# Attention with beacons, then a three-way maxout FFN: pair loads over 128 partitions, and three loads moved between queues and steps

## The chip, the cores and the metric

One Trainium2 chip; the kernel runs on one of its cores. The metric is device time in microseconds (us), read as the median of several runs of the whole kernel; lower is better. Within the core, TensorE (PE) multiplies, VectorE (DVE), ScalarE (ACT) and GpSimd (POOL) work on what it needs and leaves, and SyncE (SP) mostly issues transfers. Each engine takes its own instructions strictly in program order, so an instruction that waits holds back everything behind it on that engine. Transfers (DMAs) are issued from the queues of SP, ACT and POOL and are carried by 16 DMA engines that all queues share.

## The reference

Eight batches, eight heads, 576 tokens of width 64, and 16 beacon tokens per head that every query may see. The output of the attention, 4608 tokens by 512, goes through a maxout FFN.

```python
k_all = np.concatenate([beacon_k, k], axis=2)
v_all = np.concatenate([beacon_v, v], axis=2)
scores = scale * np.matmul(q, k_all.transpose(0, 1, 3, 2))
...
scores = np.where(causal, -1000000000.0, scores)
scores = scores - scores.max(-1, keepdims=True)
a = np.exp(scores)
a /= a.sum(-1, keepdims=True) + 1e-09
return np.matmul(a, v_all).astype(np.float32)
...
h = np.maximum(np.maximum(x @ w1, x @ w2), x @ w3)
return (h @ w_out).astype(np.float32)
```

All inputs and the output are float32 in memory. Here S is 576, Nb (beacons) 16, D 64, and the FFN goes 512 to 768 to 512.

## The kernel before

**The order is written out by hand.** The kernel turns off the scheduler's own choice of order (`manual_schedule`); what stands first in the code is issued first on its engine. The unit of attention work is a *pair* of heads: 32 pairs, four per batch. A pair's scores come in four groups (0 to 3). Two pairs make a *quad*, which is multiplied with the values in two halves (`emit_pv(quad, half)`). FFN work comes in 22 units per block of 512 tokens (`mm1_halves`, `mm1_unit`, `mm2_unit`), and `emit_ffn` slips them between the attention steps up to a running limit.

**How q and k come in.** In batch 0, halves and quads of heads are loaded (`load_half`, `load_quad`) and turned on TensorE (`turn_half`). In batches 1 to 3 (pairs 4 to 15, `B_PE = 4`) a pair is loaded in float32 by `load_pair` on SP's queue: token `6p + r` goes to partition `p` of 96, so one descriptor carries 6 tokens, 1536 bytes. POOL turns it into bf16 with two casts (`cast_pair`, `cast_piece`, line 218), TensorE turns it with 6 transposes for q and 6 for k (`turn`, line 347, each 96 columns), and the result is copied out of PSUM, k by DVE (`evac_k`, line 394) and q by ACT (`evac_q`, line 383; for pair 4 by DVE). From batch 4 on, pairs are stored in bf16 and come back through transposing DMAs; the change does not alter that route.

**How the values come in.** `load_v(b, piece)` loads a batch's values as tiles of 128 keys, descriptors of 256 bytes: piece 0 has tiles 0 to 2 and the 16 beacon rows, piece 1 has tiles 3 and 4. POOL casts them (line 275 for batch 0, line 263 later).

**Weights.** `load_w(i, ...)` (line 285) and `load_w_out` (line 290) are issued on POOL's own queue and cast from float32 to bf16 on the way. Each `load_w` is two DMAs.

**The first stage.** `start()` and the list `first_steps` set batch 0's order: `T` turns a half, `M` masks, `V` casts a value tile, `P` multiplies with the values, `F` emits FFN units, `G(p)` loads a pair behind a one-column memset on DVE that acts as a gate. `load_v(0, 1)` has such a gate too. `idle` is a number of filler transposes that `turn_half` puts before the second of its two parts, and `keep_busy` issues filler matmuls; neither result is used.

**Around the change**, POOL's order from 29 us on is: casts of pair 4, third weight (two DMAs), casts of pair 5, masks of pair 4, casts of pair 6, masks of pairs 4 and 5, cast of batch 1's first values (step (5, 0)), `load_w_out`, two masks of pair 5, cast of the other values, casts of pair 7, masks of pair 6. TensorE's order at step (6, 0) is: scores of pair 6, the product of quad 2 with the values (needs pair 5's masks), one FFN unit, the transposes of pair 7, and then the first FFN unit that reads the third weight. The output weight is first read by the first `mm2_unit`, at step (8, 0), line 620.

**SP's order** there is: pair 4, pair 5 (both gated), pair 6, batch 1's values in six DMAs, pair 7, then batch 2. A DMA of SP or ACT takes one of eight semaphores in turn, and waits for the DMA eight places before it.

```python
groups_any = [
    [(0, 0, HALF), (3, q_min[3], S)],
    [(0, HALF, S), (4, q_min[4], S)],
    [(1, q_min[1], S)],
    [(2, q_min[2], S)],
]
...
for p in range(8, B_PE * PPB):
    at_step(p - 2, 1, C(cast_pair, p, by_pool, by_pool))
```

Of the kernel before, what the change touches and what calls it, by code (L numbers as in the profile page):

```python
# [16 lines left out]
def kernel(  # L17
# [28 lines left out]

    QR = 6
    QP = S // QR
    HR = QR // 2
    HALF = S // 2  # L50

# [53 lines left out]
    def place(p):  # L105
        b, pi = divmod(p, PPB)
        return b, pi // PPQ, 2 * (pi % PPQ)
# [36 lines left out]
    qTs = [const.tile([128, S], BF16, name=f"qT{i}") for i in range(NT)]  # L144
    kTs = []
    for i in range(NT):
        z = const.tile([128, NKP], BF16, name=f"kT{i}")
        nc.vector.memset(z[:, NK:NKP], 0.0)
        nc.vector.memset(z[:, Nb + HALF : 384], 0.0)
        kTs.append(z)  # L150
# [20 lines left out]

    def load_pair(p, gate=None):
        b, g, j0 = place(p)
        hs = slice(head(g, j0), head(g, j0) + 2)
        st = new_stage(("pair", p))

        if gate:
            gate.memset(st[0:QP, 0:1], 0.0)
        for i, src in enumerate((q, k)):
            nc.sync.dma_start(  # L180
                out=st[0:QP, i * NQ2 : (i + 1) * NQ2].rearrange("p (h x) -> p h x", h=2),
                in_=src[b, hs].rearrange("h (p r) d -> p h (r d)", r=QR),
            )
# [31 lines left out]
    def cast_piece(p, i, cast):  # L215
        st = stage["pair", p]
        t16 = pair_pool.tile([QP, QR, 2, D], BF16, name=f"p16{i}")
        cast(  # L218
            t16.rearrange("p r h d -> p h r d"),
            st[0:QP, i * NQ2 : (i + 1) * NQ2].rearrange("p (h r d) -> p h r d", h=2, r=QR),  # L220
        )
        stage["pair16", p, i] = t16

    def cast_pair(p, q_cast, k_cast):
        cast_piece(p, 0, q_cast)
        cast_piece(p, 1, k_cast)
        stage.pop(("pair", p))
# [3 lines left out]
    def load_v(b, piece, gate=None):  # L231
        st = new_stage(("v", b, piece))
        if gate:
            gate.memset(st[0:QP, 0:1], 0.0)
        t_lo, t_hi = V_PIECES[piece]
        for t in range(t_lo, t_hi):
            i = t - t_lo
            dst = st[:, i * H * D : (i + 1) * H * D].rearrange("p (h d) -> p h d", h=H)
            lo = 0
            if t == 0:  # L240
                lo = Nb
                nc.sync.dma_start(
                    out=dst[0:Nb], in_=beacon_v[b].rearrange("h n d -> n h d")
                )
            t0 = k_tok[t] + lo
            n = k_rows[t] - lo
            nc.sync.dma_start(
                out=dst[lo : lo + n], in_=v[b, :, t0 : t0 + n, :].rearrange("h p d -> p h d")
            )
# [94 lines left out]
    def turn(p, i, ps):  # L344
        src = stage.pop(("pair16", p, i))
        for r in range(QR):
            nc.tensor.transpose(  # L347
                ps[:, r * QP : (r + 1) * QP],
                src[:, r].rearrange("p h d -> p (h d)"),
                ident[0:QP, 0:QP],  # L350
            )

# [29 lines left out]
    def evac_q(p, ps, copy):  # L382
        copy(
            qTs[p % NT].rearrange("d (p r) -> d p r", r=QR),
            ps.rearrange("d (r p) -> d p r", r=QR),
        )
# [5 lines left out]
    def evac_k(p, ps, copy):  # L392
        kT = kTs[p % NT]
        copy(
            kT[:, Nb:NK].rearrange("d (p r) -> d p r", r=QR),
            ps.rearrange("d (r p) -> d p r", r=QR),
        )

    def turn_apart(p, i):
        ps = ffn_psum.tile([128, S], BF16, name="fps")  # L400
        turn(p, i, ps)
        (evac_q, evac_k)[i](p, ps, by_dve)
        if i == 1:
            place_beacons(p, by_act)

    def turn_pair(p, q_copy, shared=True):
        if shared:
            ps = sc_psum.tile([128, 2, 1024], BF16, name="sc")
            banks = [ps[:, i, 0:S] for i in range(2)]
        else:  # L410
            banks = [pv_bank(i, [128, 1024], BF16)[:, 0:S] for i in range(2)]
        for i in range(2):
            turn(p, i, banks[i])
        evac_k(p, banks[1], by_dve)
        evac_q(p, banks[0], q_copy)
# [286 lines left out]
    loads = [L(load_v, 0, 0), L(load_v, 0, 1, nc.vector), L(load_beacons, 1, B_PE, bk32_1)]  # L702
# [18 lines left out]
    def start():  # L721
# [25 lines left out]
        keep_busy(3)  # L747
# [41 lines left out]
    def F(n):  # L789
# [7 lines left out]
        ((2, 0), [T(0, 1, False, None, 6), next_2, V(2), L(load_w, 0, 0, d_ff)]),  # L797
        ((3, 0), [T(1, 1, True, None, 8), M(1, 0, True), M(2, 0, True)]),
        ((0, 1), [M(0, 1)]),
        ((0, 2), [T(2, 1, False), M(3, 0, True), M(0, 2), V(3), V(4)]),  # L800
        ((0, 3), [M(0, 3, True), L(load_w, 1, 0, d_ff)]),
        ((1, 1), [P(0, 0), M(1, 1)]),
        ((1, 2), [T(3, 1, False), finish_pv, M(1, 2)]),
        ((1, 3), [P(1, 0, True), M(1, 3, True)]),
        ((2, 1), [finish_pv, G(4), cast_p]),
# [4 lines left out]
        ((3, 3), [F(2), M(3, 3), L(cast_pair, 4, by_pool, by_pool), L(load_w, 2, 0, d_ff), P(1, 1),  # L810
# [4 lines left out]
    at_step(5, 0, L(load_w_out))  # L815
    at_step(5, 1, C(cast_v, 1, 1, by_pool))
    at_step(5, 1, C(cast_pair, 7, by_pool, by_pool))
    for p in range(8, B_PE * PPB):
        at_step(p - 2, 1, C(cast_pair, p, by_pool, by_pool))
# [127 lines left out]
```

## Time and profile before

| | |
|---|---|
| median of 6 runs | 301.66 us |
| lowest and highest run | 300.61 and 307.27 us |
| the profiled execution's own time | 300.54 us |
| span of that execution in the trace | 298.8 us |
| PE busy | 282.8 us (95%) |
| PE weight loads, beside the matmuls | 153.1 us (51%) |
| DVE, ACT, POOL busy | 173.1, 146.3, 128.2 us |
| DMA moved | 50.68 MB in 85320 packets, mean 170 GB/s |
| share of packets under 512 bytes | 64416 of 85320 |

A line of the trace's timeline reads: start, length (both in us from the span's start), engine, line of the kernel, operation, output tile <- input tile, shape, count, and in brackets the idle time of the engine just before it and what ended it. A line of the list of waits reads: who waited, for whom, total us, how many times, the longest. The chain of waits is followed back from the end of the span; each piece is the work that released the next. The granted TensorE clock is full in all parts of the span.

### The profile page before, as it was taken

What the parts mean: (1) busy time and instruction counts of PE and PEld (TensorE: products, weight loads), DVE (VectorE), ACT (ScalarE), POOL (GpSimd) and SP (SyncE); (2) the same over time, 40 slices, a digit from 0 to 9 for tenths busy, and PEclk for the clock granted to TensorE, in tenths of its full rate; (3) what the DMA queues carried; (4) which work ended last, traced back from release to release, by engine and by line L of the source; (5) the groups of instructions that cost most, each with busy time, mean ns of one, the idle gap of its engine ahead of it and who ended that gap; (6) DMA issues with size and microseconds to landing.
All of it is one profiled execution on the core that took longest, in us unless ns stands there. A gap on an engine that the chain in (4) does not pass through costs nothing.

```text
span 298.8 us, 8667 instructions
## 1 busy us (share of the span) xinstructions
PE 282.8 (95%) x3571; PEld 153.1 (51%) x3601; DVE 173.1 (58%) x343; ACT 146.3 (49%) x237; POOL 128.2 (43%) x253
## 2 busy tenths in 40 slices
PE   8879977999999999999999999999999999999995
PEld 4546644554545454444545777545454554444442
DVE  3756644455767576646563757375746575284373
ACT  3685574875665465546453646364635431401300
POOL 7181856666475684456455645552233210000000
PEclk9999999999999999999999999999999999999999
DMA  8999989999999999999999999983111001103003
GB/s 146 186 184 232 216 187 265 250 224 296 231 234 240 189 312 206 194 195 318 223 186 220 316 226 186 162 263 82 42 67 76 2 3 73 69 1 128 14 0 141
DMA packets 85320, 50.68 MB, mean 170 GB/s; under 512 B 64416, under 2 KB 80032, under 8 KB 85280
## 3 DMA queue, kind: packets, MB, share of 16 engines
q1 hardware_dynamic: 80672, 45.76, 69.1%
q0 software_dynamic: 4048, 4.03, 8.2%
q8 instruction: 28, 0.46, 0.7%
q10 hardware_dynamic: 560, 0.33, 0.5%
q14 instruction: 12, 0.10, 0.1%
HBM read 35.13 MB, written 14.22 MB: 165 GB/s over the span
## 4 chain that ended last, share of the span: by engine, by line
PE 81%; DMA 9%; POOL 3%; DVE 2%; ACT 2%; issue 1%; SPq 0%; POOLq 0%; DVEq 0%
PE fps L584 31%; PE sc L584 12%; PE pv L524 11%; PE fps L620 11%; PE sc L452 8%; PE sc L620 4%; DMA st<-in_v_dram 4%; DMA quad<-in_k_dram 3%; DMA st<-in_k_dram 2%; PE sc L347 2%; ACT at_sb L461 1%; DVE xT L556 1%; POOL v_sb L263 1%; POOL quad L209 1%; DVE y L628 1%
## 5 line engine op out<-in xcount | busy, mean ns | idle before, releaser
L461 ACT ACTIVATE at_sb<-sc 128x928 bf16<-128x928 f32 (+5 forms) x128 | 103.8, 861 | 83.9 <-PE sc L452 83.2
L584 PE MATMUL fps<-xT,w_sb 128*128 128x512 bf16 (+1 forms) x464 | 106.4, 356 | 2.1 <-issue 0.8
L480 POOL TENSOR_SCALAR_AFFINE_SELECT at_sb<-at_sb 128x256 bf16<-128x256 bf16 (+2 forms) x148 | 53.9, 383 | 97.2 <-ACT at_sb L461 97.2
L584 PEld LDWEIGHTS <-w_sb 128*128 128x128 bf16 x672 | 61.7, 98 | 65.3 <-issue 12.2
L594 DVE TENSOR_TENSOR hT<-hT,fps 128x512 bf16<-128x512 bf16 x70 | 48.0, 687 | 29.4 <-PE fps L584 29.0
L218 POOL CAST p<-st 96x768 bf16<-96x768 f32 x56 | 44.7, 822 | 1.1 <-DVE hT L613 0.6
L584 PE MATMUL sc<-xT,w_sb 128*128 128x512 bf16 (+1 forms) x187 | 42.9, 356 | 0.1
L452 PE MATMUL sc<-qT,kT 64*128 64x288 bf16 (+5 forms) x400 | 35.9, 277 | 2.4 <-ACT at_sb L461 2.0
L620 PE MATMUL fps<-w_out_sb,hT 128*128 128x512 bf16 x143 | 34.6, 379 | 0.9 <-issue 0.6
L620 PEld LDWEIGHTS <-hT 128*128 128x128 bf16 x210 | 19.8, 98 | 24.1 <-DVE hT L594 2.1
L594 DVE TENSOR_TENSOR hT<-hT,sc 128x512 bf16<-128x512 bf16 x32 | 22.0, 688 | 16.9 <-PE sc L584 11.3
L628 DVE COPY y<-fps 128x512 f32<-128x512 f32 x25 | 17.3, 692 | 23.5 <-PE fps L620 23.5
L592 DVE CAST hT<-fps 128x512 bf16<-128x512 f32 x32 | 22.1, 692 | 12.3 <-PE fps L584 12.2
L556 DVE TENSOR_TENSOR xT<-pv,recip 128x288 bf16<-128x288 f32 (+2 forms) x93 | 27.3, 349 | 2.7 <-ACT recip L546 2.7
L524 PE MATMUL pv<-at_sb,v_sb 128*32 128x288 bf16 (+5 forms) x1376 | 28.7, 229 | 0.0
L452 PEld LDWEIGHTS <-kT 64*128 64x128 bf16 x400 | 14.4, 94 | 26.7 <-issue 22.1
L524 PEld LDWEIGHTS <-v_sb 128*32 128x32 bf16 (+1 forms) x1408 | 24.4, 96 | 2.0 <-issue 0.6
L524 PE MATMUL pv<-at_sb,ones 128*32 128x288 bf16 (+4 forms) x500 | 17.5, 256 | 2.5 <-POOL at_sb L480 2.4
L263 POOL CAST v_sb<-st 128x1536 bf16<-128x1536 f32 (+2 forms) x21 | 18.4, 893 | 3.0 <-DMA st<-in_v_dram 3.0
L544 ACT ACTIVATE lnd<-pv 128x288 f32<-128x288 f32 x31 | 12.9, 416 | 10.0 <-PE pv L524 10.0
L524 PEld LDWEIGHTS <-ones 128*32 128x32 bf16 (+2 forms) x512 | 10.9, 95 | 9.8 <-issue 8.2
L592 ACT CAST hT<-sc 128x512 bf16<-128x512 f32 x6 | 3.5, 586 | 23.7 <-PE sc L584 23.7
(74 smaller groups left out, 163.0 us busy)
## 6 DMA issues: line engine op xcount, KB each, us to landing
out_dram<-y SPq DMA_DIRECT2D x35, 256.0 KB, 3.2
st<-in_q_dram SPq DMA_DIRECT2D x28, 288.0 KB, 5.8
st<-in_k_dram SPq DMA_DIRECT2D x28, 288.0 KB, 6.4
st<-in_v_dram SPq DMA_DIRECT2D x24, 256.0 KB, 5.6
w_sb<-in_moe_w_dram POOLq DMA_DIRECT2D x6, 384.0 KB, 7.3
q_dram<-p SPq DMA_DIRECT2D x16, 144.0 KB, 2.9
k_dram<-p SPq DMA_DIRECT2D x16, 144.0 KB, 2.9
st<-in_v_dram SPq DMA_DIRECT2D x8, 224.0 KB, 6.2
```

What stands on the lines that cost most here:

```text
L218: cast(t16.rearrange("p r h d -> p h r d"), st[0:QP, i * NQ2 : (i + 1) * NQ2].rearrange("p (h r d) -> p h r d", h=2, r=QR),)
L263: cast(v_sb[0:n, t:t1].rearrange("p t h d -> p (t h d)"), st[0:n, (t - t_lo) * H * D : (t1 - t_lo) * H * D],)
L452: nc.tensor.matmul(ps[:, e, off : off + q1 - q0], kT[hs, 128 * t : 128 * t + 128], qT[hs, q0:q1], start=True, stop=True, tile_position=(64 ...
L461: nc.scalar.activation(out=both_heads(p, gi), in_=ps[:, :, 0 : g_width(p, gi)], func=AF.Exp, scale=scale)
L480: nc.gpsimd.affine_select(out=view, in_=view, compare_op=ALU.is_ge, fill=0.0, base=x0, pattern=[[0, 2], [1, hi - lo]], channel_multiplier=-1,)
L524: nc.tensor.matmul(ps[bank][32 * j : 32 * j + 32, lo + q0 - qa : lo + qb - qa], lhsT, at_view(PPQ * quad + j // 2, t, j % 2, q0, qb), star ...
L556: nc.vector.tensor_mul(xT[:, 2 * g + part - 1, c0 + ca : c0 + cb], ps[bank][:, lo : lo + cb - ca], recip[:, ca:cb],)
L584: nc.tensor.matmul(ps[:, o0 : o0 + n], w_in[i][:, ct, 128 * ft : 128 * (ft + 1)], xT[:, ct, x0 : x0 + n], start=(ct == 0), stop=(ct == n_c ...
L592: (by_act if alone[0] else by_dve)(h, ps)
L594: nc.vector.tensor_max(h, h, ps)
L620: nc.tensor.matmul(ps, hT[:, ft, 128 * tt : 128 * (tt + 1)], w_out_sb[:, ft, :], start=(ft == 0), stop=(ft == n_ft - 1),)
L628: nc.vector.tensor_copy(y, ps)
```

## The change

Pairs of batches 1 to 3 are loaded over 128 partitions: tokens 0 to 511 as `4p + r` (1024 bytes a descriptor), and the remaining 64 tokens of q and of k in one square, q on partitions 0 to 63, k on 64 to 127 (256 bytes a descriptor). That is 4 DMAs for a pair in place of 2, 3 casts in place of 2, 9 transposes of 128 columns in place of 12 of 96, and one copy more out of PSUM: the square's two halves go to the ends of q and k in one strided copy, for which qT and kT become parts of one tile. q's copy has 512 columns in place of 576.

The third weight is issued at step (4, 1), behind the masks of pair 4, in place of step (3, 3); the output weight at step (6, 0) in place of (5, 0). In batch 0 the second value tile is issued on ScalarE's queue, and in every batch the beacon rows come behind the first value tile. P(1, 0) moves behind the scores (2, 1). The fillers grow: one matmul, and 2 + 8 + 8 transposes.

```diff
+    WR = 4
+    WIDE = 128 * WR
+    REST = S - WIDE
...
-    qTs = [const.tile([128, S], BF16, name=f"qT{i}") for i in range(NT)]
-    kTs = []
...
+    qkTs = [const.tile([128, S + NKP], BF16, name=f"qkT{i}") for i in range(NT)]
+    qTs = [z[:, 0:S] for z in qkTs]
+    kTs = [z[:, S : S + NKP] for z in qkTs]
...
+    def load_wide(p, gate=None):
+        b, g, j0 = place(p)
+        hs = slice(head(g, j0), head(g, j0) + 2)
+        st = new_stage(("pair", p))
+
+        if gate:
+            gate.memset(st[:, 0:1], 0.0)
+        W = 2 * WR * D
+        for i, src in enumerate((q, k)):
+            nc.sync.dma_start(
+                out=st[:, i * W : (i + 1) * W].rearrange("p (h x) -> p h x", h=2),
+                in_=src[b, hs, 0:WIDE].rearrange("h (p r) d -> p h (r d)", r=WR),
+            )
+        for i, src in enumerate((q, k)):
+            nc.sync.dma_start(
+                out=st[REST * i : REST * (i + 1), 2 * W : 2 * W + 2 * D].rearrange("p (h d) -> p h d", h=2),
+                in_=src[b, hs, WIDE:S].rearrange("h p d -> p h d"),
+            )
...
+    def cast_wide(p, cast):
+        st = stage.pop(("pair", p))
+        t16 = pair_pool.tile([128, 2 * QR, 2, D], BF16, name="p16")
+        W = 2 * WR * D
+        for i in range(2):
+            cast(
+                t16[:, WR * i : WR * (i + 1)].rearrange("p r h d -> p h r d"),
+                st[:, i * W : (i + 1) * W].rearrange("p (h r d) -> p h r d", h=2, r=WR),
+            )
+        cast(t16[:, 2 * WR].rearrange("p h d -> p (h d)"), st[:, 2 * W : 2 * W + 2 * D])
+        stage["wide16", p] = t16
...
-    def load_v(b, piece, gate=None):
+    def load_v(b, piece, gate=None, queues=None):
...
+            (queues[i] if queues else nc.sync).dma_start(
+                out=dst[lo : lo + n], in_=v[b, :, t0 : t0 + n, :].rearrange("h p d -> p h d")
+            )
...
     def turn(p, i, ps):
-        src = stage.pop(("pair16", p, i))
-        for r in range(QR):
+
+        src = stage["wide16", p]
+        slots = [(r, WR * i + r) for r in range(WR)] + ([(WR, 2 * WR)] if i == 1 else [])
+        for r, slot in slots:
             nc.tensor.transpose(
...
     def evac_k(p, ps, copy):
...
         copy(
-            kT[:, Nb:NK].rearrange("d (p r) -> d p r", r=QR),
-            ps.rearrange("d (r p) -> d p r", r=QR),
+            kTs[p % NT][:, Nb : Nb + WIDE].rearrange("d (p r) -> d p r", r=WR),
+            ps[:, 0:WIDE].rearrange("d (r p) -> d p r", r=WR),
         )
+        step = S + Nb
+        x0 = S + NKP - 2 * step
+        copy(
+            qkTs[p % NT][:, x0:].rearrange("d (i x) -> d i x", i=2)[:, :, WIDE - x0 : S - x0],
+            ps[:, WIDE : WIDE + 2 * REST].rearrange("d (i x) -> d i x", i=2),
+        )
...
-    loads = [L(load_v, 0, 0), L(load_v, 0, 1, nc.vector), L(load_beacons, 1, B_PE, bk32_1)]
+    loads = [L(load_v, 0, 0, None, (nc.sync, nc.scalar, nc.sync)), L(load_v, 0, 1, nc.vector), L(load_beacons, 1, B_PE, bk32_1)]
...
-        keep_busy(3)
+        keep_busy(4)
...
-        ((2, 0), [T(0, 1, False, None, 6), next_2, V(2), L(load_w, 0, 0, d_ff)]),
+        ((2, 0), [T(0, 1, False, None, 8), next_2, V(2), L(load_w, 0, 0, d_ff)]),
...
-        ((0, 2), [T(2, 1, False), M(3, 0, True), M(0, 2), V(3), V(4)]),
+        ((0, 2), [T(2, 1, False, None, 8), M(3, 0, True), M(0, 2), V(3), V(4)]),
...
-        ((1, 2), [T(3, 1, False), finish_pv, M(1, 2)]),
-        ((1, 3), [P(1, 0, True), M(1, 3, True)]),
-        ((2, 1), [finish_pv, G(4), cast_p]),
+        ((1, 2), [T(3, 1, False, None, 8), finish_pv, M(1, 2)]),
+        ((1, 3), [M(1, 3, True)]),
+        ((2, 1), [P(1, 0, True), finish_pv, G(4), cast_p]),
...
-        ((3, 3), [F(2), M(3, 3), L(cast_pair, 4, by_pool, by_pool), L(load_w, 2, 0, d_ff), P(1, 1),
+        ((3, 3), [F(2), M(3, 3), L(cast_pair, 4, by_pool, by_pool), P(1, 1),
...
-    at_step(5, 0, L(load_w_out))
+    at_step(4, 1, L(load_w, 2, 0, d_ff))
...
+    at_step(6, 0, L(load_w_out))
```

## The prediction, on record before the changed kernel was run

> **What bounds the kernel now.** I read the page's table of busy time first, then the chain of waits, then the timelines of TensorE, GpSimd and SyncE where the chain leaves TensorE.
>
> ```profile
> PE 282.8 (95%) x3571; PEld 153.1 (51%) x3601; DVE 173.1 (58%) x343; ACT 146.3 (49%) x237; POOL 128.2 (43%) x253
> ...
> PE 81%; DMA 9%; POOL 3%; DVE 2%; ACT 2%; issue 1%; SPq 0%; POOLq 0%; DVEq 0%
> ```
>
> TensorE does the work that ends last: in the timeline four 512-column matmuls of the FFN take 0.86 us, one behind the other. So a change helps only where TensorE stands still, or where it gets less to do. From 60 us to the end its gaps over 0.15 us are some 0.16 each. The chain leaves it for long in one place, before 51 us:
>
> ```profile
> 23.49 7.44 DMA st<-in_k_dram
> 30.94 11.59 DMA st<-in_v_dram
> 42.68 1.46 POOL v_sb L263
> 44.14 0.79 POOL w_out_sb L290
> 44.94 0.77 POOL at_sb L480 x2
> ```
>
> Batch 1's values land at 42.6 us, POOL casts them, issues the output weight, and only then masks pair 5, for which TensorE waits. The same in the timelines (POOL, then PE, then SP):
>
> ```profile
> 31.75 1.08 POOL L285 DMA_DIRECT2D w_sb<-in_moe_w_dram  x2
> ...
> 38.69 1.01 POOL L480 TENSOR_SCALAR_AFFINE_SELECT at_sb<-at_sb 128x224 bf16<-128x224 bf16 x3 [0.41 <-ACT at_sb L461]
> 42.68 1.46 POOL L263 CAST v_sb<-st 128x1536 bf16<-128x1536 f32 x1 [2.98 <-DMA st<-in_v_dram]
> ```
> ```profile
> 45.41 0.55 PE L524 MATMUL pv<-at_sb,ones 128*32 128x176 bf16 x6 [2.35 <-POOL at_sb L480]
> ...
> 47.64 0.43 PE L347 MATMUL sc<-ident,p 96*128 96x96 bf16 x6 [0.24 <-POOL p L218]
> 48.50 0.43 PE L347 MATMUL sc<-ident,p 96*128 96x96 bf16 x6 [0.44 <-POOL p L218]
> ```
> ```profile
> 29.33 11.59 SPq L247 DMA_DIRECT2D st<-in_v_dram  x5
> 40.97 1.01 SPq L180 DMA_DIRECT2D st<-in_q_dram  x1
> ```
>
> Five value DMAs need 11.59 us to be issued, while the third weight, issued at 31.75, is moving. In the trace's packets its 256 are carried from 34.6 to 41.0 us and take 64.2 us of engine time, over 16 engines 4.0 us. From 37 to 38 us the engines began 66 of them and no packet of the values. That is what the change attacks.
>
> **The third weight moves (step (4, 1)).** Without its 4.0 us the first values land at 42.55 - 4.0 = 38.6. POOL reaches the weight's issue at 38.3 (end of pair 4's masks, 37.52 + 0.76), spends 1.08 on it, masks pair 5 until 40.4 and casts the values until 41.9 (1.46): it no longer waits for them. Pair 5's last two groups leave ACT at about 41.7 and 42.4, POOL masks them by 42.8, and the wait of 2.35 at 45.41 is gone. Next in line is pair 7. POOL casts the other values (1.16) by 44.0 and pair 7 by 45.5; TensorE, which ended pair 7's transposes at 48.93, could end them at 46.0. That is the upper end, a gain of 2.9. It needs pair 7 in SBUF by 45.2, and now the third weight runs against pair 7. Its first packets came 1.3 us (first weight) to 2.9 us (third) behind the issue, so from 39.6 to 41.2. If pair 7 is shut out as the values were, it lands when values, pair 7 and weight are all through. Pair 6 lands at 35.6 in the trace; a 256 KB value tile lands 1.1 to 1.2 us behind the one before (at 61 to 63 us), 4.6 tiles make 5.3; pair 7 takes 2.3 (two landings, 1.15 apart, in pairs 4 to 6); with the weight's 4.0 that is 47.2, and POOL's last cast (0.29, below) lets TensorE end at 48.0: a gain of 0.9, the lower end. It can be better, since SP now gets to pair 7 some 2 us earlier (its issue at 40.97 stood behind the values' issue, and from 41 to 42 us the engines were busy 0.48). I take 2.1 between the two: the three weights' issues are followed by gaps nearer 2.9 than 1.3 when the queue is full, which favours pair 7.
>
> **The output weight (step (6, 0)).** It is issued behind pair 6's masks (1.01), so at about 46.7 instead of 44.08, and took 13.7 us to land. TensorE reads it at 60.72, and 2.1 earlier if the gain holds: 58.6. With 13.7 it would land at 60.4, a wait of 1.8; that is one end. Of the 13.7, 4.3 passed before its first packet and 8.5 with packets alternating with pair loads of 1536 bytes (78 ns in the median, its own 97). Two thirds of a pair's packets now have 1024 bytes and one third 256 (18 ns); scaled by bytes from 78, 52 and 18 average 41, and 48 rounds of 97 + 41 give 6.6: landing at 57.9, no wait, the other end. I take 0.2, near the second end, since that one has the packets that the new kernel moves.
>
> **Loads over 128 partitions.** Per pair and engine: before 24 packets of 78 ns, 1.87 us; after 32 of 52 and 16 of 18, 1.95. Nothing gained by that; I take 0 (-0.3 to +0.3 for each of pairs 4 to 7), hidden behind the prefetch of 8 stage tiles later on (pair 8 landed at 49.7, cast at 52.4). SP issues two DMAs more per pair, 0.45 us each: 0.9 us for 12 pairs, covered as long as four issues (1.8) stay under a pair's 2.3. The casts: 610 ns for 128x512 (row of the values' cast) twice and, from 610 and 1459 for 1536 columns, about 290 for 128 columns: 1.51 against 2 x 822 = 1.64.
>
> Two sentences of the Trainium skill speak against this part. "DMA: Bandwidth & Descriptors", section "Rules for kernel authors", advises to merge small transfers, since under 64 KB overhead is most of the cost; the two new DMAs have 32 KB each. The trace agrees half: a 32 KB beacon DMA takes 4.9 us to land and a 256 KB tile 5.6, but several are in flight at once. By the rule, with its fixed cost as an estimate of 2 us for each, pair 7 would come 4 us later and the sum would be a loss of about 2.
>
> **Transposes and copies.** Filler transposes have 128 columns too: 6 take 0.51 and 8 take 0.62, so 55 ns each; 96 columns: 6 take 0.43 and 12 take 0.68, so 42. Nine of 55 are 495 ns, twelve of 42 are 504: nothing. DVE's copy: 754 ns for 576 columns and 454 for 288, so 687 for 512 and 287 for 128: 0.22 more per pair, and ACT (640 for 576, 400 for 288, so 587 for 512) starts behind it. Both lie under FFN units that follow the transposes (98.39, 3.83 us), except for pair 7, where scores waited 0.35 for ACT's copy. I take +0.1 (0 to 0.2 for one pair; 9 x 0.17 = 1.5 if the cover were gone).
>
> **The first 23 us.** A value tile of 256 KB goes to ACT's queue, its issue (0.45) under ACT's wait of 2.35 before 4.44. Then two queues of values alternate with the quads of q and k on POOL's queue, where before it was one; TensorE waits for a quad three times (0.49 at 9.05, 0.39 at 12.04, 0.27 at 14.72). Lower end 0, upper end the tile's own 1.2. Against it, scores (2, 1) ahead of P(1, 0) give ACT back its 0.43 of idle before 20.38. The fillers, 18 x 55 ns and one matmul of 0.3, lie in those waits and in 0.38 and 0.93 for ACT; the cost is their 1.3 if the waits were gone. Sum 0.1 (-0.4 to +0.9). If the delay is large, values and first weight overlap more, POOL's last cast of values and behind it the second weight come later.
>
> The same page, same section, has it that spreading DMAs over several queues gains no bandwidth, only issue time. By that rule the move is worth SP's 0.44 us of issue, which nothing waits for, and the sum would be unchanged.
>
> **The sum.** -2.1 + 0.2 + 0 + 0.1 + 0.1 = -1.7 on the profiled execution: 300.54 - 1.7 = 298.8 (span 297.1). That execution lies 1.1 under the median of the runs shown, 301.66; I keep the distance and forecast a median of 301.66 - 1.7, rounded to 299.9.
>
> **Rivals.**
> 1. *The stall only changes its place.* Pair 7 lands at 47.2 (gain 0.9), the output weight is issued 1.5 later and lands late by 1, the first 23 us lose 0.5: 301.66 - 0.9 + 1.0 + 0.5, about 302.2, taken as 301.0 to 302.9. For it: DMA share is about 1.0 or over from 20 to 200 us save 41 to 46. Against it: just that stretch is free to be used.
> 2. *Slower: the output weight.* If pair 7 lands at 47.2, POOL casts until 47.5, masks until 48.5 and only then issues it; with 13.7 it lands at 62.2, 1.5 behind the 60.72 of before, with all earlier gains swallowed, and with the start's 0.9 not recovered separately. It decides from an issue after 47.0 (60.72 - 13.7). Time 301.66 + 1.5 to 3, about 303.5. For it: a slack of only 3.0 before (landed 57.7). Against it: the shorter packets beside it.
> 3. *The move doesn't do what it says:* the values don't land earlier because SP's eight semaphores hold pair 6 until pair 4 has landed (29.7; before, it was issued at 26.95). Then pair 6 is 1 us late, the gain 1 smaller: 300.9. It counts with rival 1.
>
> **How the numbers follow.** Forecast (a gain of 1.5 to 3.2, 298.5 to 300.2) 0.50; rivals 1 and 3 0.25; rival 2 0.25. A measurement of this kernel tells about 0.5% (1.5 us) from no change: faster 0.52, with a little of rival 3; same 0.22; slower 0.26. The forecast's own range is 298.5 to 300.3; reaching to the other cases, 298.2 to 303.2.
>
> **What would show it.** Right: POOL's cast at L263 begins near 40.4 with no wait for a DMA, PE's wait of 2.35 is gone, and pair 7's transposes end before 47. Wrong: a wait of PE over 1 us on a weight (the first `mm1_unit` with the third, or the first `mm2_unit`), on pair 7's casts, or quads that land over 1 us later; and any new gaps behind 60 us, where I cost the whole change at nothing.

## The result and the profile after

| | before | after |
|---|---|---|
| median of all runs | 301.37 us (69 runs) | 307.1 us (34 runs) |
| lowest run | 299.75 us | 301.26 us |
| ratio after / before | | 1.0068 (95% interval 1.0045 to 1.0092) |
| the profiled execution's own time, its span | 300.54, 298.8 us | 305.86, 304.1 us |

The forecast was 299.9 (298.2 to 303.2); the change makes the kernel slower, by 0.7% in the comparison. Executions of both kernels scatter upward by several us, of the new one more often, and the ratio leaves disturbed ones out, so it is smaller than the distance of the medians.

The page of the kernel after: busy time, granted clock in 40 slices, and the chain of waits by engine.

```profile
PE 286.2 (94%) x3554; PEld 155.5 (51%) x3584; DVE 173.9 (57%) x355; ACT 145.6 (48%) x237; POOL 125.8 (41%) x265
...
PEclk9997999999997999999999999999999999999999
...
PE 78%; DMA 9%; POOL 4%; DVE 3%; ACT 2%; SPq 2%; issue 2%; POOLq 0%; DVEq 0%; ACTq 0%
```

TensorE's share of the chain fell from 81 to 78%, POOL's rose from 3 to 4, and SP's queue, which had none, has 2. The clock was lowered in two slices. First the place that the change aimed at, in the timelines of POOL and of TensorE after:

```profile
41.41 1.08 POOL L322 DMA_DIRECT2D w_sb<-in_moe_w_dram  x2
42.49 1.02 POOL L526 TENSOR_SCALAR_AFFINE_SELECT at_sb<-at_sb 128x224 bf16<-128x224 bf16 x3
43.45 1.46 POOL L300 CAST v_sb<-st 128x1536 bf16<-128x1536 f32 x1
```
```profile
45.96 0.41 PE L570 MATMUL pv<-at_sb,ones 128*32 128x288 bf16 x12
...
49.84 0.61 PE L630 MATMUL fps<-xT,w_sb 128*128 128x512 bf16 x2 [0.76 <-DMA w_sb<-in_moe_w_dram]
```

The cast of batch 1's first values waits for nothing, and the 2.35 us at this product (45.41 before) are gone. But TensorE comes to this place 3.3 us later than before (26th exponent in the table below), and the weight itself is now waited for. The 3.3 us come from the start (POOL, then TensorE):

```profile
17.48 0.60 POOL L312 CAST v_sb<-st 128x512 bf16<-128x512 f32 x1
22.27 0.61 POOL L312 CAST v_sb<-st 80x512 bf16<-80x512 f32 x1 [4.19 <-DMA st<-in_v_dram]
22.83 1.08 POOL L322 DMA_DIRECT2D w_sb<-in_moe_w_dram  x2
```
```profile
24.39 0.52 PE L570 MATMUL pv<-at_sb,ones 128*32 128x208 bf16 x6 [1.92 <-POOL at_sb L526]
```

POOL stands 4.19 us at the cast of the last value tile (it landed at 22.2, before at 18.1); behind it are the second weight (18.87 before) and the masks for which TensorE waits. The clock is at half in the 3.4 us that follow. The second loss lies where the prediction saw nothing (POOL, then TensorE):

```profile
80.61 0.29 POOL L250 CAST p<-st 128x128 bf16<-128x128 f32 x1
88.10 0.61 POOL L740 CAST bk<-bk 64x512 bf16<-64x512 f32 x1 [7.19 <-DMA bk<-in_beacon_k_dram]
88.66 1.01 POOL L526 TENSOR_SCALAR_AFFINE_SELECT at_sb<-at_sb 128x224 bf16<-128x224 bf16 x3
89.62 1.75 POOL L261 CAST p<-st 96x768 bf16<-96x768 f32 x2
91.33 0.76 POOL L526 TENSOR_SCALAR_AFFINE_SELECT at_sb<-at_sb 128x256 bf16<-128x256 bf16 x2
```
```profile
91.78 0.56 PE L570 MATMUL pv<-at_sb,ones 128*32 128x176 bf16 x6 [2.40 <-POOL at_sb L526]
...
95.36 1.88 PE L630 MATMUL fps<-xT,w_sb 128*128 128x512 bf16 x6
```

POOL waits 7.19 us for the beacons of batches 4 to 7 (before 3.00, at 83.55), the masks behind it are late, TensorE waits, and then runs at half clock (six of these matmuls take 1.46 us at full clock). Why the beacons are late is seen in SP's timeline, first before, then after:

```profile
61.86 1.01 SPq L180 DMA_DIRECT2D st<-in_q_dram  x1
62.91 0.45 SPq L180 DMA_DIRECT2D st<-in_k_dram  x1
...
66.95 0.31 SPq L180 DMA_DIRECT2D st<-in_k_dram  x1
...
78.81 2.26 SPq L296 DMA_DIRECT2D bk<-in_beacon_k_dram  x4
```
```profile
64.63 0.47 SPq L185 DMA_DIRECT2D st<-in_q_dram  x1
65.15 0.47 SPq L185 DMA_DIRECT2D st<-in_k_dram  x1
65.66 0.60 SPq L190 DMA_DIRECT2D st<-in_q_dram  x1
66.31 0.60 SPq L190 DMA_DIRECT2D st<-in_k_dram  x1
...
75.73 0.61 SPq L190 DMA_DIRECT2D st<-in_k_dram  x1
...
82.75 3.29 SPq L333 DMA_DIRECT2D bk<-in_beacon_k_dram  x4
```

Pairs 12 to 15 took SP 5.4 us (61.86 to 67.26: eight loads and one store) and take 11.7 (64.63 to 76.34: sixteen loads and one store, each issue 0.47 to 0.61 us long but for one of 1.44). The turn of the eight semaphores is not what holds SP here: at each of these seventeen issues the DMA eight places before had landed at least 0.5 us earlier. The transfers have room meanwhile, as the table by stage says for 70 to 80 us (the last two numbers: share of the 16 DMA engines, GB/s), before and after:

```profile
70.00:80.00 10.00, 9.78 (x103) 4.57 (x104) 7.36 (x16) 6.14 (x10) 6.24 (x13) 1.00 1.13 284
```
```profile
70.00:80.00 10.00, 9.79 (x100) 4.67 (x101) 7.51 (x16) 6.24 (x10) 5.50 (x13) 1.00 0.72 216
```

To see where time is lost, take one thing that every kernel does equally often: ScalarE's 128 exponents. The table has, for each profiled execution, how much later (or earlier, -) than in the kernel before the 16th, 26th, 28th, 50th and 52nd of them ended; the times before were 28.86, 43.97, 51.97, 89.59 and 93.88 us. From the 52nd to the 128th the difference moves by 0.05 us at most in every kernel: all that is lost or gained is so before the 52nd.

| kernel | 16th | 26th | 28th | 50th | 52nd | median, its before | ratio (95%) |
|---|---|---|---|---|---|---|---|
| after, first profile | 3.43 | 3.27 | 0.38 | 0.54 | 5.69 | 307.1, 301.37 | 1.0068 (1.0045-1.0092) |
| r0_after | 0.67 | 0.90 | -1.52 | -1.36 | 1.75 | 305.47, 300.95 | 1.0114 (1.0064-1.0164) |
| e1_v_on_act | 5.14 | 5.15 | 3.70 | 3.70 | 4.29 | 305.72, 300.95 | 1.0160 (1.0116-1.0204) |
| e2_weights | 3.08 | 3.09 | 4.85 | 6.20 | 6.20 | 302.66, 300.95 | 1.0033 (1.0003-1.0063) |
| e3_wide | -0.34 | 2.33 | 0.98 | 1.13 | 4.38 | 305.56, 300.95 | 1.0140 (1.0108-1.0172) |
| e4_bk_early | 0.99 | 0.83 | -0.95 | 0.59 | 3.89 | 307.13, 301.4 | 1.0154 (1.0094-1.0214) |
| e5_v_on_sp | 0.21 | 0.05 | 0.78 | 0.95 | 5.00 | 302.73, 301.4 | 1.0054 (1.0024-1.0083) |
| e6_split | 1.71 | 1.71 | 3.85 | 4.68 | 4.67 | 303.23, 301.4 | 1.0058 (1.0017-1.0100) |
| e7_wide_weights_bk | 3.72 | 3.56 | 3.01 | 3.58 | 8.91 | 308.28, 301.4 | 1.0187 (1.0144-1.0230) |
| e8_rest_by_batch | -0.30 | -0.46 | -0.55 | 1.24 | 1.23 | 301.76, 302.91 | 0.9972 (0.9937-1.0007) |
| e9_casts_later | -0.36 | -0.52 | -0.30 | 2.40 | 2.39 | 301.8, 302.91 | 0.9982 (0.9939-1.0026) |
| e10_both | -0.05 | -0.21 | -0.95 | -0.78 | -0.80 | 301.28, 302.91 | 0.9915 (0.9863-0.9966) |
| e11_third_earlier | 6.75 | 6.69 | 4.46 | 4.62 | 4.61 | 301.23, 301.91 | 0.9965 (0.9937-0.9992) |
| e12_pair8_held | 3.69 | 3.54 | 3.15 | 5.07 | 5.06 | 299.46, 301.31 | 0.9935 (0.9902-0.9969) |
| e13_both_again | 0.10 | -0.06 | -2.28 | -2.12 | -2.13 | 301.13, 301.31 | 0.9956 (0.9918-0.9993) |

### The profile page after: what moved, and what is told of

It is laid out like the page before. It is cut to its first block, busy times and chain, and to the rows that moved or that the text cites. A ratio compares the mean times of both kernels' runs of the same rounds, so it can differ in the third digit from the quotient of the medians.

```text
span 304.1 us, 8661 instructions
## 1 busy us (share of the span) xinstructions
PE 286.2 (94%) x3554; PEld 155.5 (51%) x3584; DVE 173.9 (57%) x355; ACT 145.6 (48%) x237; POOL 125.8 (41%) x265
## 4 chain that ended last, share of the span: by engine, by line
PE 78%; DMA 9%; POOL 4%; DVE 3%; ACT 2%; SPq 2%; issue 2%; POOLq 0%; DVEq 0%; ACTq 0%
PE fps L630 29%; PE sc L630 12%; PE pv L570 11%; PE fps L666 10%; PE sc L498 7%; PE sc L666 4%; DMA quad<-in_k_dram 3%; DMA st<-in_v_dram 3%; DMA w_sb<-in_moe_w_dram 3%; PE fps L649 2%; ACT at_sb L507 1%; POOL at_sb L526 1%; PE sc L386 1%; SPq L333 1%; DMA bk<-in_beacon_k_dram 1%
## 5 line engine op out<-in xcount | busy, mean ns | idle before, releaser
L630 PE MATMUL fps<-xT,w_sb 128*128 128x512 bf16 (+1 forms) x464 | 107.5, 358 | 2.9 <-issue 1.0
L498 PE MATMUL sc<-qkT 64*128 64x288 bf16 (+5 forms) x400 | 35.9, 278 | 1.4 <-ACT at_sb L507 1.2
L638 DVE CAST hT<-fps 128x512 bf16<-128x512 f32 x32 | 22.1, 691 | 12.1 <-PE fps L630 11.9
L498 PEld LDWEIGHTS <-qkT 64*128 64x128 bf16 x400 | 14.6, 94 | 25.8 <-issue 21.6
L261 POOL CAST p<-st 96x768 bf16<-96x768 f32 x32 | 25.5, 822 | 0.1
L570 PE MATMUL pv<-at_sb,ones 128*32 128x288 bf16 (+4 forms) x500 | 18.2, 256 | 4.8 <-POOL at_sb L526 4.7
```

The source lines that it names most:

```text
L261: cast(part.rearrange("p r h d -> p h r d"), st[0:QP, i * NQ2 : (i + 1) * NQ2].rearrange("p (h r d) -> p h r d", h=2, r=QR),)
L498: nc.tensor.matmul(ps[:, e, off : off + q1 - q0], kT[hs, 128 * t : 128 * t + 128], qT[hs, q0:q1], start=True, stop=True, tile_position=(64 ...
L570: nc.tensor.matmul(ps[bank][32 * j : 32 * j + 32, lo + q0 - qa : lo + qb - qa], lhsT, at_view(PPQ * quad + j // 2, t, j % 2, q0, qb), star ...
L630: nc.tensor.matmul(ps[:, o0 : o0 + n], w_in[i][:, ct, 128 * ft : 128 * (ft + 1)], xT[:, ct, x0 : x0 + n], start=(ct == 0), stop=(ct == n_c ...
L638: (by_act if alone[0] else by_dve)(h, ps)
```

## The experiments: the change and its parts

**r0_after**, the changed kernel once more.

> The changed kernel once more, beside the parts of it. From the first comparison (ratio 1.0068, 1.0045 to 1.0092) it should be 1.5 to 3 us above the kernel before in the median, and the profile should show TensorE waiting some 2 us near 24 us and some 2.5 us between 88 and 93 us. If those two waits were accidents of one profiled execution, they are absent here and the time is within 1 us of before.

This profile has a full clock throughout, and the late beacons and TensorE's wait are there again:

```profile
89.52 0.56 PE L570 MATMUL pv<-at_sb,ones 128*32 128x176 bf16 x6 [2.23 <-POOL at_sb L526]
...
91.84 1.46 PE L630 MATMUL fps<-xT,w_sb 128*128 128x512 bf16 x6
```

The wait near 24 us is not: there the loss is 0.7 to 0.9. So the step from the 50th to the 52nd exponent costs 3.1 us by itself, and 5.15 with the half clock of the first profile; the start costs 0.7 to 0.9 by itself and 3.4 in the first profile, with its wait at 24 us and the half clock behind it.

**e1_v_on_act**, the kernel before with the queue of one tile changed.

```diff
...
-    loads = [L(load_v, 0, 0), ...
+    loads = [L(load_v, 0, 0, None, (nc.sync, nc.scalar, nc.sync)), ...
```

> Kernel before with one edit: batch 0's second value tile on ScalarE's queue. Theory (the start's loss comes from this queue): batch 0's last value tile lands near 22 us in place of 18.1, POOL waits for it and issues the second weight near 22.8, TensorE waits 1.5 to 2 us near 24 us and everything behind is 1.5 to 3.4 us later; the wait of 2.35 at 45 us remains or shrinks by what was lost; time +1 to +2.5 us. Rival (the loss of the start comes from the fillers and from P(1, 0) behind the scores (2, 1)): last tile near 18, no wait at 24 us, time within 0.7 us of before.

The last value tile lands at 20.2 (18.1 before) and POOL issues the second weight at 20.85 (18.87), so this part of the mechanism is there; TensorE's wait near 24 us is not. The loss is larger than forecast: in this profile the clock is at half from 11.9 to 29.0 us, behind an idle of 1.36 at the second quad. Five of its six times are over 304.8, above what either side forecast. One of them, 305.76, has a mean granted clock of 0.999 (a figure that leaves out the time before the clock first comes to full), so a later fall of the clock is not shown to be the whole of the excess.

**e2_weights**, the kernel before with the two weights moved.

```diff
-        ((3, 3), [..., L(cast_pair, 4, by_pool, by_pool), L(load_w, 2, 0, d_ff), P(1, 1),
+        ((3, 3), [..., L(cast_pair, 4, by_pool, by_pool), P(1, 1),
-    at_step(5, 0, L(load_w_out))
+    at_step(4, 1, L(load_w, 2, 0, d_ff))
+    at_step(6, 0, L(load_w_out))
```

> Kernel before with the third weight at step (4, 1) and the output weight at (6, 0) and nothing else. Theory (this part alone does what it says): the wait of 2.35 at 45 us is gone, no wait of TensorE over 1 us takes its place, time -1.0 to -2.4 us. Rival A (the weights' move is what makes pairs 8 to 13 late, and the cast of batches 4 to 7's beacons on POOL with them): pair 10 is issued near 50 us in place of 45.3, POOL waits near 88 us for the beacons over 5 us, TensorE waits over 2 us near 91 us, time 0 to +2. Rival B (the output weight is late without the shorter packets of the wide loads): TensorE waits 1 to 2 us at the first mm2_unit.

Neither: no gain, no wait near 90 us, none at the first `mm2_unit`. The stall went to the third weight itself (TensorE's timeline):

```profile
51.17 0.60 PE L584 MATMUL fps<-xT,w_sb 128*128 128x512 bf16 x2 [2.10 <-DMA w_sb<-in_moe_w_dram]
53.68 1.03 PE L584 MATMUL fps<-xT,w_sb 128*128 128x512 bf16 x2 [1.91 <-DMA w_sb<-in_moe_w_dram]
```

Issued at 41.3, it lands at 53.6, with pairs 7 to 9 beside it, all issued ahead. TensorE came 3.1 us late here, with the clock at half from 18.0 to 28.2 us.

**e3_wide**, the kernel before with `load_wide`, `cast_wide` and the new `turn`, `evac_q` and `evac_k` of the change's diff, and nothing else.

> Kernel before with the wide loads, 9 transposes and their copies alone: four DMAs for a pair, weights and batch 0 as before. Theory (four DMAs for a pair and only eight under way hold the loads back): pairs 10 to 13 land 2 to 4 us later than before, batches 4 to 7's beacons land near 87 us in place of 83.4, POOL waits for them 5 to 7 us, TensorE waits 1.5 to 3 us between 88 and 93; time +1 to +3 us. Rival (the loads fall behind only because of the third weight's move): beacons land within 1 us of 83.4, no wait of TensorE over 1 us behind 60 us, time within 0.7 us of before.

The theory's lateness is there and the rival falls: beacons at 87.8, POOL waits 6.47, TensorE 2.73 at 92.1. The ratio, 1.0140, is some 4 us, above the 1 to 3 expected. The profile shows a second cost, which was not expected (POOL, then TensorE):

```profile
40.46 0.29 POOL L250 CAST p<-st 128x128 bf16<-128x128 f32 x1 [3.77 <-DMA st<-in_k_dram]
```
```profile
40.81 0.23 PE L387 MATMUL pv<-ident,p 128*128 128x128 bf16 x1 [2.66 <-POOL p L250]
```

Pair 6's last square, 32 KB issued at 30.7, right behind the third weight's first DMA (30.2 in this kernel), lands at 40.3, while its 256 KB parts, issued ahead of the weight, were there by 33. In this profile wide loads and an early third weight don't go together: the weight's move is needed to undo a cost of the loads.

**e4_bk_early**, the changed kernel with the four beacon DMAs ahead of pair 12's.

```diff
-        if b == B_PE:
-            loads.append(L(load_beacons, B_PE, B, bk32))
+        if b == B_PE - 1:
+            loads.append(L(load_beacons_and_pair, b * PPB))
...
```

> Changed kernel; the four DMAs of batches 4 to 7's beacons are issued ahead of pair 12's, in place of behind batch 3's values. Theory (the loss near 90 us comes from these beacons landing behind loads that SP issues too slowly, and from POOL, which stands at their cast): they land before 72 us, POOL's wait of 7 us near 86 us and TensorE's wait of 2.2 to 2.4 near 90 us are gone, no wait over 1 us comes in their place; about 3 us less than the changed kernel in runs without a lower clock, so a ratio to before of 0.997 to 1.003. Rival (all loads are late, the beacons only show it first): POOL waits as long for the next pairs' loads, the gain is under 1 us, ratio 1.006 to 1.012.

The rival holds. The beacons are there when POOL comes (its cast at 80.91 has no wait), and POOL stands at the next load instead, pair 16's q:

```profile
89.41 0.82 POOL L261 CAST p<-st 96x768 bf16<-96x768 f32 x1 [6.45 <-DMA st<-in_q_dram]
```

TensorE waits 2.78 at 91.65, and the ratio, 1.0154, is above what either side expected. So it isn't the beacons: SP's whole queue is behind.

**e5_v_on_sp**, the changed kernel with the value tile back on SP's queue.

```diff
-    loads = [L(load_v, 0, 0, None, (nc.sync, nc.scalar, nc.sync)), ...
+    loads = [L(load_v, 0, 0), ...
```

> Changed kernel with batch 0's second value tile back on SP's queue; the beacon rows stay behind the first tile. Theory (the start's loss comes from the ScalarE queue): the second k half and the first quads land within 0.3 us of before, the waits of 0.79 at 8 and 1.01 at 10 us shrink to under 0.5, at 31 us the kernel is within 0.4 us of before; 1 us less than the changed kernel, more where a lower clock was set off at the start; ratio to before 1.002 to 1.008. Rival (fillers, P(1, 0) behind the scores (2, 1), or the order of the beacon rows): the start stays 0.7 us or more behind before, ratio as the changed kernel's, 1.006 to 1.012.

The start is within 0.2 us of before (16th and 26th exponent), with all the other edits of the start in it: the queue alone made that loss. (e8, e9, e10 and e13 below keep the tile on SP's queue, and are within 0.4 us at the 16th exponent; e4, with the tile on ScalarE's, lost 1.0.) Last tile 18.1, second weight issued at 18.82. But now that TensorE comes in time, the third weight's move brings nothing, and from the 26th to the 28th exponent 0.7 us are lost:

```profile
47.56 0.61 POOL L246 CAST p<-st 128x512 bf16<-128x512 f32 x1 [2.16 <-DMA st<-in_k_dram]
```

Pair 7's k was issued at 38.61, 0.4 us behind the weight (38.19), and landed at 47.5. In r0_after it was issued at 38.19, ahead of the weight (39.04), and landed at 42.7. 1.3 us in the order of the two issues go with 4.8 us in the landing.

**e6_split**, the kernel before with each pair load cut by head.

```diff
+            cuts = (0, 1, 2) if p < B_PE * PPB else (0, 2)
+            for h0, h1 in zip(cuts, cuts[1:]):
...
```

> Kernel before with each pair load of batches 1 to 3 cut by head: four DMAs for a pair in place of two, descriptors of 1536 bytes, casts, transposes and copies as before. Theory (the number of DMAs that SP has to issue holds the loads back, not the shape of their descriptors): SP issues pairs 12 to 15 in over 9 us in place of 5.4, batches 4 to 7's beacons land at 86 us or later in place of 83.4, POOL waits over 5 us for them, TensorE 1.5 to 3 us near 91; time +2 to +4 us. Rival (the descriptors of 256 and 1024 bytes): beacons within 1 us of 83.4, no wait of TensorE over 1 us behind 60 us, time within 1 us of before.

Inconclusive. SP took 10.7 us for pairs 12 to 15 and the beacons landed at 87.9, as the theory has it; but TensorE was itself 4.7 us late by then (a wait of 1.67 at 46 us for batch 1's values, one of 2.18 at 52 for pair 7's k, and three stretches at half clock), POOL waited only 2.77 and TensorE not at all.

**e7_wide_weights_bk**: the edits of e2, e3 and e4 together, the start as before.

> Kernel before with the wide loads and both weights' moves, batch 0 as before, and the beacons of batches 4 to 7 ahead of pair 12. Theory (the third weight's move is worth 2.4 us and only the start and the beacons ate it up): nothing lost by 31 us, the wait of 2.35 at 45 us gone, no wait of TensorE over 1 us behind 60 us; 1.5 to 2.5 us less than before, ratio 0.992 to 0.995. Rival (parts of the change need each other: the weight's move pays only with the new start): a new wait of over 1 us for the third weight or for pair 7, ratio 0.998 to 1.005.

Far off (six runs, 306.1 to 311.9). In its profile the clock first came to full at 17.5 us (six fillers take 0.82 us until then, 0.51 in e3), in the kernel before at 6.8; the third weight is waited for (2.25 at 51.8), and pair 16's q is late as in e4 (TensorE waits 3.15 at 95 us). Why all its runs took so long, one profile can't tell; that stays open.

## The experiments: what takes the losses away

**e8_rest_by_batch**: on top of e5, the short pieces of a batch in two DMAs.

```diff
+        if p % PPB == 0:
+            rests[b] = rest_pool.tile([128, H, D], FP32, name="rest")
+            for i, src in enumerate((q, k)):
+                nc.sync.dma_start(
+                    out=rests[b][REST * i : REST * (i + 1)],
+                    in_=src[b, :, WIDE:S].rearrange("h p d -> p h d"),
+                )
...
+        cast(t16[:, 2 * WR], rests[b][:, h0 : h0 + 2])
...
```

> Changed kernel with the value tile back on SP's queue, and the last 64 tokens of q and of k of a whole batch loaded by two DMAs (512 descriptors of 256 bytes each) with the batch's first pair, in place of two with every pair: 10 DMAs for a batch in place of 16, with the same bytes in descriptors of the same sizes. To make room, the three float32 beacon tiles share one. Theory (what holds the loads back is the number of DMAs that SP issues, some 0.55 us each, back to back from 63 to 76 us): SP issues pairs 12 to 15 in under 8 us, batches 4 to 7's beacons land at 84.5 us or earlier, TensorE's wait near 90 us is gone or under 0.5, and so is the one of 0.6 to 2.4 for pair 7's square near 47; time 298.5 to 300.5, ratio 0.990 to 0.998. Rival (the short descriptors cost the transfers their rate, whoever issues them): beacons at 86 us or later, TensorE waits 1.5 to 3 us near 91, ratio 1.002 to 1.010.

SP needs 7.9 us for pairs 12 to 15, a store and one long issue of 2.15 included (the DMA eight places before that one had landed 2.4 us earlier, so it wasn't its semaphore; what held it isn't known); the beacons land at 83.7 and TensorE doesn't wait (POOL, then TensorE at the product that waited in the others):

```profile
83.83 0.61 POOL L745 CAST bk<-bk 64x512 bf16<-64x512 f32 x1 [2.22 <-DMA bk<-in_beacon_k_dram]
```
```profile
89.14 0.40 PE L575 MATMUL pv<-at_sb,ones 128*32 128x288 bf16 x12
```

The same bytes in descriptors of the same sizes, six DMAs fewer for a batch: their number was it, not the shape of their descriptors. TensorE came as late here (1.24 at the 50th) as in e3 (1.13) and e5 (0.95), which both waited, so this isn't the cover that e6 had. The interval lies wholly under e5's, though the two ran on different chips, each beside its own runs of the kernel before. What remains is a wait of 0.56 and 2.19 for the third weight near 46 to 48 us, since now pair 7 is the first.

**e9_casts_later**: on top of e5, two casts on POOL behind pair 13's.

```diff
-    at_step(B_PE * PPB - 6, 1, L(by_pool, bk16, bk32))
+    at_step(B_PE * PPB - 5, 0, next_load)
+    at_step(B_PE * PPB - 5, 1, L(cast_pair, B_PE * PPB, by_pool, by_pool), L(by_pool, bk16, bk32))
...
```

> Changed kernel with the value tile back on SP's queue, and the casts of batches 4 to 7's beacons and of pair 16 on GpSimd moved behind pair 13's cast, to step (11, 1); all loads as they were. Theory (TensorE waits near 91 us because GpSimd stands at a cast whose load is late, with masks queued behind it): the loads stay as late (beacons at 86 to 88 us), but GpSimd's wait is under 3 us in place of 6 to 7 and TensorE's near 91 us under 0.5; 2 to 4 us less than with the value tile alone put back, ratio 0.993 to 0.999. Rival (every load behind is as late, and the wait moves on to pairs 13 to 17 or the stores of batch 4): a wait of over 1.5 us within 15 us behind, ratio 1.002 to 1.008.

The beacons still land at 87.6, POOL gets to them at 92.85 and waits for nothing, and the step from the 50th to the 52nd exponent is 0. TensorE came 2.4 us late, 1.4 more than in e5, but that isn't what hid the wait: POOL stood idle for 4.21 us, up to 88.98, waiting for ScalarE's output to mask, so it had time to spare. The late loads cost time only because POOL stood at them with masks queued behind.

**e10_both**, the edits of e8 and e9 together, and the same kernel once more beside e12, **e13_both_again**:

> The two together: last tokens by batch, and the casts of pair 16 and of the beacons at step (11, 1). If the loads by batch alone take the wait near 90 us away, this one equals them within 0.5 us; if either leaves a part of it, this one is the fastest. 298 to 300 us, ratio 0.988 to 0.996. Rival (what was gained before 60 us is limited by something else than SP and GpSimd, the transfers themselves): a wait of TensorE over 1 us remains between 60 and 110 us, ratio over 0.998.

> The last tokens by batch and the two casts at step (11, 1) once more, beside the kernel that holds pairs 8 to 10 back, on one chip. It should repeat its ratio of 0.9915 (0.986 to 0.997); a ratio over 0.998 would say that the first one was luck.

0.9915 and 0.9956, both intervals under 1: faster than the kernel before by 0.4 to 0.9% in the comparison (the medians of all runs differ by 1.6 and 0.2 us). In e13's profile, with a full clock, the third weight's move is worth what was predicted of it: -2.28 at the 28th exponent, and nothing is given back (span 296.6, before 298.8). The wait at 45 us has shrunk to this:

```profile
47.18 0.61 PE L635 MATMUL fps<-xT,w_sb 128*128 128x512 bf16 x2 [1.43 <-DMA w_sb<-in_moe_w_dram]
```

In e10's it was 2.63, and the gain 0.95.

**e11_third_earlier**, the third weight at step (4, 0), on top of e10_both.

```diff
-    at_step(4, 0, C(cast_pair, 6, by_pool, by_pool))
-    at_step(4, 1, L(load_w, 2, 0, d_ff))
+    at_step(4, 0, L(load_w, 2, 0, d_ff), C(cast_pair, 6, by_pool, by_pool))
```

> Last tokens by batch and the two casts at step (11, 1), as in the run before, and the third weight at step (4, 0), ahead of pair 6's casts, in place of (4, 1): about 2 us earlier on GpSimd's queue. In the run before TensorE waited 2.63 for this weight at 48.5 us, with batch 1's values and pair 7 in time. Theory (the weight's landing is now what ends last there, with 2 us to spare for values and pair 7): that wait shrinks to 0.5 to 1.2, no other over 0.7 comes before 60 us; 1 to 2 us less, ratio 0.985 to 0.991. Rival (values, pair 7 and weight share the transfers, so that one of them is late whatever the order): values or pair 7 come late instead, a wait of 1 us or more at 45 to 47 us, ratio 0.991 to 0.996.

No better than e10_both (0.9965, and medians 301.23 and 301.28). Its profile ran at half clock from 10.6 to 31.1 us, so TensorE came 6.7 us late, and its small waits for pair 7 (0.34 and 0.78) and none for the weight decide nothing.

**e12_pair8_held**, on top of e10_both, pairs 8 to 10 held back behind the cast of batch 1's first values.

```diff
...
-        ((3, 2), [F(1), finish_pv, next_7, M(3, 2)]),
+        ((3, 2), [F(1), finish_pv, next_4, M(3, 2)]),
...
+    at_step(5, 0, L(cast_v, 1, 0, by_pool), next_5)
...
+        gate = nc.gpsimd if b == 2 else None
```

> As with the last tokens by batch and the two casts at step (11, 1), and pairs 8 to 10 are held back: pair 8's load is gated by a one-column memset on GpSimd behind the cast of batch 1's first values, so that their DMAs no longer move beside the third weight. Theory (it is these pairs, issued at 37.7 to 45 us, that stretch the weight): the weight lands at 46.5 us or earlier in place of 48.5, TensorE's wait for it falls from 2.6 to under 0.8, pair 7 and the values stay in time, no wait over 1 us behind; 1.5 to 2.5 us less than without the hold, ratio to before 0.980 to 0.988. Rival (values, pair 7 and weight alone fill the transfers up to 47 to 48 us, so the gain there is bound whatever else is moved): weight at 47.5 or later, wait of 1.8 or more, ratio 0.990 to 0.996, or the pairs held back come late themselves and TensorE waits over 1 us for pair 8 or 9.

The rival holds in the profile: the weight took 10.3 us from issue (41.67) to landing (51.94), against 10.5 in e10 and 9.0 in e13, though no pair behind 7 was issued before 45.26; TensorE waited 1.91. The ratio, 0.9935, is that of the kernel without the hold within the intervals. In the trace's packets the weight moves alone from 45 to 48 us, and what was left of it then moves beside pair 8 until 51.94; TensorE was 3.5 us late, with the clock at half from 10.3 to 20.6 us. So pairs 8 to 10 explain at most the end of the weight's 10 us. That values, pair 7 and weight bound this stretch by themselves, and the order only chooses which of them is late, fits all these runs, but no run has the three alone.

## Why the prediction was wrong

- **Third weight, -2.1 (0.9 to 2.9).** The mechanism was right: the wait for the values is gone in every kernel that has the move. In the changed kernel the size came out too, but by luck: from the 26th to the 28th exponent it gains 2.9 and 2.4, in profiles in which TensorE had come 3.3 and 0.9 late, which leaves the loads time. With TensorE in time, e5 and e9 lost 0.7 and 0.2 there, and e8, e10 and e13 gained 0.1, 0.7 and 2.2 (in e5, e8 and e9 the clock fell to half here). The weak step is "I take 2.1 between the two ... which favours pair 7": it was a race between SP's issue and POOL's, decided by 0.4 us in e5 and e8, and when pair 7 won it, the weight was late (e8, e10, e13), which the prediction named only as a sign of error. Rival 1, the stall that changes place, was the better description.
- **Output weight, +0.2.** Right at its second end: issued at 49.50, landed at 59.48, 10.0 us in place of 13.7, and TensorE at the first `mm2_unit` doesn't wait. Rival 2 falls; e2 has no such wait either.
- **Wide loads, "I take 0 ... hidden behind the prefetch of 8 stage tiles".** This is the step that lost the case. The issues were counted ("covered as long as four issues (1.8) stay under a pair's 2.3"), but against the transfer of one pair, and not along SP's queue: four issues are 2.1 to 2.2 us, sixteen and a store 11.7. What was taken as 0 cost 3.1 to 3.3 us. And the cover was never looked at where it ends. The timelines of before had the lines that price it (POOL, then TensorE):

```profile
83.55 0.61 POOL L694 CAST bk<-bk 64x512 bf16<-64x512 f32 x1 [3.00 <-DMA bk<-in_beacon_k_dram]
...
86.87 0.76 POOL L480 TENSOR_SCALAR_AFFINE_SELECT at_sb<-at_sb 128x256 bf16<-128x256 bf16 x2
```
```profile
87.90 0.41 PE L524 MATMUL pv<-at_sb,ones 128*32 128x288 bf16 x12
```

  POOL already stood at this load, and behind it the first of two masks ends at 87.25 (half of 0.76 behind 86.87) for matmuls that start at 88.1 (half of 0.41 behind 87.90): some 0.9 us to spare. In e3 the masks start at 91.69, 4.8 later, and TensorE is 1.1 later: 4.8 - 1.1 - 0.9 = 2.8, and its wait is 2.73. In all, the step to the 52nd exponent costs 3.1 to 3.3 us (r0, e3, e4); e8 and e9 each take it away.
- **The rule that was set aside.** The Trainium skill, "DMA: Bandwidth & Descriptors", section "Rules for kernel authors", advises to merge transfers under 64 KB. e8 merges eight of 32 KB into two of 128 KB and agrees: POOL's wait for the beacons falls from 6.25 (e5) to 2.22. The loss of "about 2" that the rule was worth in the prediction was nearer the truth than the 0 taken, though it came at another place, through issues and not at pair 7.
- **Transposes and copies, +0.1.** Right as far as the rows show: 9 transposes take 0.68 us where 12 took 0.68, and a pair's casts 1.45 in place of 1.64.
- **The first 23 us, +0.1 (-0.4 to +0.9).** The upper end was the value: 0.7 to 0.9. In r0_after it lies where the term put it, at loads of q and k that land later (TensorE waits 0.79 at 8.08 and 1.01 at 10.43). The chain behind it was named ("POOL's last cast of values and behind it the second weight come later") but not priced; TensorE waited for it in the first profile alone (1.92 at 24.39). e5 shows that the queue is all of it.
- **The clock.** It was not in the sum at all. Where it fell to half for 3.413 us behind a wait, that cost up to 1.7 us (half of the stretch) on top of the wait's own length, twice in the first profile. That the clock of the kernel before is full in all parts holds from 6.8 us on, where its record begins.

Two slips of arithmetic change nothing: the second end of the output weight adds up to 58.5, not 57.9 (46.7 + 4.3 + 6.6, and the 0.9 that 4.3 and 8.5 leave of 13.7), and 301.66 - 1.7 is 299.96.

For the undisturbed profile r0_after the corrected sum is +0.9 - 2.4 + 3.1 = +1.6; its time is 301.91 against 300.54, +1.4. The three terms are read off this same profile, so they say where its time went and test nothing. It is also the lowest of six runs: what the other five, 304.08 to 311.3, lost beyond it, no trace shows.

## What to carry to other kernels

Cost a transfer twice: by its bytes, and by the time its issue takes in the queue of the engine that issues it, added up over all that stands in that queue, until the first place where something waits for a load already in the profile of before. A gain upstream eats the slack of every load behind it, so look up how long each later load still had. An in-order engine that casts loads and also masks for TensorE should meet a late load only behind the masks (e9).

## What the runs showed of the hardware

- Loads of SP's queue that were issued shortly behind the first DMA of a cast-loading weight on POOL's queue took long to land: pair 7's k landed 8.9 us after its issue when it came 0.4 us behind the weight (e5), and 4.5 us after it when it came 0.9 us ahead (r0_after). A piece of 32 KB, 0.5 us behind, took 9.6 us (e3).
- The granted clock fell to half in stretches of 3.413 us or multiples (up to 20.48, e11), in the first profile behind idles of TensorE of only 1.92 and 2.40 us. Behind idles of 2.63 (e10) and 2.78 (e4, at 91.65) it stayed full. In e11 and e12 it fell at 10.6 and 10.3 us, and behind the start-up no idle over 0.75 us had gone before, so that such a gap is what sets it off is not shown. The Trainium skill, "TensorE: Matmul & The Clock Gate", "Part 1: The HAM clock gate", has a free-running window of 3413 ns, with which the lengths agree, and has the clock fall after at least one idle window of about 3.4 us. Here it fell without an idle of that length, in some executions and not in others; the measurement decides.
